# Fourier mixing and a gated feed-forward layer on one core: row E of batch 0 in four column tiles, sines loaded earlier, most weight pieces converted inside the steps

## The chip, the cores and the metric

The kernel runs on one core of a Trainium2 chip. Times are device microseconds of that core. Five engines work side by side, each through its own instructions in order: PE (TensorE, matmuls), ACT (ScalarE), DVE (VectorE), POOL (GpSimd) and SP (SyncE, which here only issues transfers). What one engine needs from another is guarded by semaphores.

## The reference

```python
x: (8, 3008, 256) float32
X = real(fft(fft(x, axis=1), axis=2))             # per batch
t = X.reshape(24064, 256)
out = (sigmoid(t @ w_gate) * (t @ w_val)) @ w_out  # w_gate, w_val: 256 x 1536; w_out: 1536 x 256
```

The three weight matrices arrive as 64-bit floats, because the random float32 values are scaled by a float64 number. The kernel turns them into float32 itself, with integer operations on the two 32-bit halves of each number.

## The kernel before

**The transform.** For one batch, positions 0 to 3007 are folded by symmetry, so that a cosine and a sine sum over a table (`ST[0]`, loaded by `load_table`) give everything: `pk` (cosine part), `qk` (sine part), each 128 features by 1505 frequencies, and one more row for the feature in the middle (feature 128 of 256), called row E here. The table comes in four transfers: two of cosines, two of sines. A sum is made by `seq_group`: twelve matmuls of about 377 columns for `pk` (two blocks, six table slices each), twelve for `qk`. An ACT copy and two DVE additions (`places`) per block bring it out of PSUM.

Row E of batch 0 is made by `seq_group` with `what` = 2. Its left operand is one column broadcast to 128 columns, so the row comes out in all 128 partitions, as tile `ek`. For batches 1 to 7 the rows come out of `e_sums`: seven columns in each of four column tiles of the array, written as one small tile `er`, stored to the DRAM tensor `ed`, and read back by `e_rows` as a broadcast to 128 partitions.

**The weights.** The feature transform is merged into `w_gate` and `w_val`, so each needs the conversion first and four matmuls with the table `dt` afterwards. The conversion is cut into 18 pieces of 512 KB, listed in `jobs` as (matrix, chunk): matrix 0 is `w_gate`, 1 is `w_val`, 2 is `w_out`. A piece goes through:

- `weight_load(j)`: one transfer on SP's queue. Pieces from number `KEEP` = 10 on use three raw buffers in turn, so the load of piece j+3 waits until piece j is converted.
- `weight_parts(j)`: two ACT operations.
- `weight_join(j)`: three DVE operations and then one addition on POOL.
- `weight_use(j)`: for `w_gate` and `w_val` the merge (`merge`): four matmuls into `ps`, two ACT copies into `G2` and `G1`, and two small transfers of row 0 of `G2` into `ge`. For `w_out` it lists the additions of `forms(g)` (`W_SUMS`, `W_COPIES`), which make the 15 weight blocks of one group of three feature tiles. They run on POOL for group 0 and on DVE for the others.

**The steps.** After the head the kernel runs 576 steps: 8 batches, 6 chunks of 252 frequencies, 12 feature tiles of 128. Step i issues, on every engine, in this order: `front_a(i)` (PE: `G1` with `pk`; in steps 0 to 4 of batch 0 also `G2` with row E, which lies as one row of an otherwise zero tile); `part(i)` (from step 5 to 11 two DVE operations that add `ge` times row E, else one ACT operation); `gate_a(i-1)` and `gate_b(i-1)` (ACT sigmoids, three DVE operations, and on POOL seven sums if (i-1) mod 3 is 1, six if it is 2); then the pieces of this step: `pre` (joins of this step, parts of the next step's joins) and `use`, and one entry of the `forms` list; `back` (PE: five matmuls of 168 columns with the weight blocks, from step 5 on); `front_b(i)` (PE: `G2` with `qk`); then what is in `side` for this step, the piece loads among it. Piece chunk c belongs to steps 2c and 2c+1 of the first twelve: `front_a(2c)` reads `G1` of both pieces of chunk c, and from step 5 on `part(2c)` reads their `ge`.

There is no planner: the order on each engine is the order of the calls (`manual_schedule`), and three tuples of step numbers say where the pieces go. Transfers take eight semaphores in turn, and a transfer also waits for the one that used its semaphore before.

Of the kernel before, what the change touches and what calls it, by code (L numbers as in the profile page):

```python
# [7 lines left out]
F32 = mybir.dt.float32  # L8
# [36 lines left out]

NQ = 6
NP = 126  # L50
HP = 64
# [3 lines left out]
              (15, 4, 6, 1)),  # L55
          2: ((11, 8, 11, 0), (12, 8, 12, 0), (9, 5, 9, 0), (10, 10, 5, 0), (16, 2, 11, 0),
              (16, 9, 16, 0))}
W_SUMS = (((1, 3), (5,), 1, 6), ((6, 7), (0, 2), 0, 8), ((4,), (8, 9), 0, 10), ((6,), (2, 3), 1, 12),
          ((0, 2), (1, 3), 0, 14), ((0,), (7,), 1, 16))
W_COPIES = ((2, -1), (0, 1), (4, 1), (5, 1))  # L60

PRODUCTS = ((0, 12), (1, 11), (4, 6), (6, 10), (2, 13), (5, 4), (13, 0),
# [15 lines left out]
def kernel(  # L78
# [10 lines left out]
    nc = tc.nc  # L89
    B, _, _, _, D = xf.shape  # L90
    F = moe_w_gate.shape[1]
    P = 128
# [35 lines left out]
    def mm(o, l, r, start, stop):  # L128
        nc.tensor.matmul(o, l, r, start=start, stop=stop, skip_group_check=True)  # L129
# [72 lines left out]


    assert NPR == 6
    jobs = [(0, 0), (1, 0), (0, 1), (1, 1), (2, 0), (0, 2), (1, 2), (2, 1), (0, 3), (1, 3), (0, 4), (2, 2),
            (1, 4), (0, 5), (1, 5), (2, 3), (2, 4), (2, 5)]
    RAW, WS = {}, {}
    shared = {}
    KEEP = 10
# [47 lines left out]
    def weight_parts(j):  # L257

        if j in RAW:
            raw, ws = RAW[j], WS[j]  # L260
            lo, hi = raw[:, :, :, 0], raw[:, :, :, 1]
            nc.scalar.activation(ws, hi.bitcast(F32), AF.Abs)
            nc.scalar.activation(lo, lo.bitcast(U32), AF.Copy, scale=2.0 ** -29)
# [83 lines left out]
    def fold_ops(b, nq):  # L347
# [58 lines left out]
            first(pool, 2, 3, qs[1])  # L406
            ops += [lambda: half1(qs[0]), lambda: half2(qs[1])]
        for blk, (v, r) in enumerate(parts):
            W[b, blk] = (v[:, :, 0:HD], r[:, :, 0:HD],
                         v[:, :, HD : HD + 1].to_broadcast([v.shape[0], NQ, P]))  # L410
        return ops


# [40 lines left out]

    def seq_start(b):
        PQE[b] = [pqp.tile([P, NK + 1], F32, name=name, tag=name) for name in ("pk", "qk")]
        if not b:
            PQE[b].append(op.tile([P, NK + 1], F32, name="ek", tag="os"))
        for t in PQE[b]:
            nc.vector.memset(t[:, NK:], 0.0)  # L460

    def seq_group(b, blk, what, other=None):
        return half(lambda q: W[b, blk][what][:, q, :], PQE[b][what], blk, what == 1, other)
# [9 lines left out]
        tt(x8[:, :, 1], x8[:, :, 0], x8[:, :, 2], op=ALU.add)  # L473
        tt(x8[:, :, 3], x8[:, :, 0], x8[:, :, 2], op=ALU.subtract)

    def e_sums():


        ps = bank("pe", 0)
        m = B - 1  # L480
        at_ = lambda blk, par: slice((2 * blk + par) * TB, (2 * blk + par) * TB + m)
        for q in range(0, NQ, 2):
            for blk in range(2):
                c0, n = ((0, NE), (NE, NO))[blk]
                for par in range(2):
                    mm(ps[at_(blk, par), 0:n], x8[:, :, 1 + 2 * blk, q + par],
                       ST[0][0:NP, 0, q + par, c0 : c0 + n], q == 0, q == NQ - 2)
        er = op.tile([P, NK + 1], F32, name="er", tag="os")[0:m]
        nc.vector.memset(er[:, NK:], 0.0)
        a = evp.tile([P, NE], F32, name="a", tag="a")[0:m]  # L490
        e1 = evp.tile([P, NE], F32, name="a", tag="a")[0:m]
        nc.scalar.copy(a, ps[at_(0, 1), 0:NE])
        nc.scalar.copy(e1[:, 0:NO], ps[at_(1, 0), 0:NO])

        def rest():
            places(er, 0, True, a, ps[at_(0, 0), 0:NE])
            nc.scalar.copy(a[:, 0:NO], ps[at_(1, 1), 0:NO])  # L497
            places(er, 1, False, e1[:, 0:NO], a[:, 0:NO])
            nc.scalar.dma_start(out=ed[1:], in_=er)
        return rest  # L500


# [40 lines left out]
    def part(i):  # L543

        pqe, ks, n, f, _ = cut(i)
        AP[i] = app.tile([P, 2, CH], F32, name="ae", tag="ae")[:, :, 0:n]
        if not N1 <= i < NFT:
            nc.scalar.activation(AP[i], PF[i], AF.Copy, scale=2.0)  # L548
            return
        for g in range(2):  # L550
            nc.vector.scalar_tensor_tensor(out=AP[i][:, g], in0=pqe[2][:, ks],  # L551
                                           scalar=ge[:, g, f : f + 1], in1=PF[i][:, g],
                                           op0=ALU.mult, op1=ALU.add)

# [131 lines left out]
    for j in range(2):  # L686
        weight_load(j)
    load_x(0)
    for _ in load_table(0, NQ // 2):
        pass  # L690
    for j in range(2, 5):
        weight_load(j)
    sines = load_table(1, NQ // 2)
    next(sines)
    for j in range(5, 7):
        weight_load(j)
# [16 lines left out]

    e0 = shared["qk"][:, 4 * WC : 4 * WC + CH]
    nc.gpsimd.memset(e0, 0.0)
    other = {(0, 0): (4, None), (0, 1): (4, None), (0, 2): (0, 1), (1, 2): (2, 3)}
# [36 lines left out]
    at(N1 - 1, lambda: nc.vector.tensor_copy(PQE[0][1][0:1, 0:CH], PQE[0][2][0:1, 0:CH]))  # L753


    i0 = NFT
# [7 lines left out]
    for i, f in enumerate(mirror_tables()):  # L764
        at(2 * i0 - 2 + i, f)
    at(3 * i0, e_fold)
    at(3 * i0 + 4, lambda: e_sums()())
    at(3 * i0 + 6, table_again)
    for i in range(i0, count, i0):
        at(i - 8, lambda i=i: e_rows(i))  # L770

# [99 lines left out]
```

## Time and profile before

| what | value |
|---|---|
| median of 3 runs | 1973.83 us (1973.28 to 1974.29) |
| the profiled execution itself | 1973.76 us |
| its span, first to last instruction | 1972.0 us |
| PE busy in the span | 1935.8 us, 98% |
| first matmul of the cosine sums | 21.39 us |
| last matmul of the sine sums ends | 46.99 us |
| second half (`front_b`) of step 0, 4, 8, 12 starts | 53.49, 70.60, 93.73, 110.19 us |
| steps from 12 on | about 3.12 us each |

PE is named by the instructions that it executes; one matmul of the program is two records in the trace. Idle time before an instruction stands in brackets with the instruction or transfer that ended it. Everything that the change touches lies in the first 120 us; from step 12 on PE has hardly a gap.

### The profile page before, as it was taken

Reading aid. Unit: us, or ns where it says so; the run is one execution under the profiler, and the core shown is the slowest. Engines: PE = TensorE matmul, PEld = TensorE weight load, DVE = VectorE, ACT = ScalarE, POOL = GpSimd, SP = SyncE. Lnnn points to the kernel's source line nnn. Section 1 sums busy time; section 2 is a strip of 40 time slices with the busy share of each in tenths; the row PEclk is TensorE's granted clock in tenths of the full one; section 3 lists DMA queues with packets and bytes.
Section 4 is the critical chain, followed back from the end, with each engine's and each line's share of the span. In section 5 each row is a group of like instructions: output and inputs, shape, how many; then the busy total and the mean of one; then the engine's idle time right before and its main releaser. Section 6 shows DMA issues by size and latency. Waiting matters only on the chain.

```text
span 1972.0 us, 34403 instructions
## 1 busy us (share of the span) xinstructions
PE 1935.8 (98%) x11252; PEld 1792.4 (91%) x11252; DVE 1511.7 (77%) x3170; ACT 1339.5 (68%) x3108; POOL 1625.0 (82%) x2843
## 2 busy tenths in 40 slices
PE   6999999999999999999999999999999999999997
PEld 4889889999999899998999989999899999999997
DVE  6888778886787677786778867787678776777777
ACT  3567657766777577775777757777577766777775
POOL 3779888997889788996889868998688996777776
PEclk9999999999999999999999999999999999999999
DMA  8363412212022121212012021211210110011011
GB/s 271 86 134 94 138 52 85 51 22 78 14 51 54 17 76 17 72 31 78 14 28 78 14 78 25 47 48 24 78 19 14 21 20 14 14 20 22 14 19 27
DMA packets 171584, 101.41 MB, mean 51 GB/s; under 512 B 133904, under 2 KB 163218, under 8 KB 168602
## 3 DMA queue, kind: packets, MB, share of 16 engines
q1 hardware_dynamic: 169434, 98.64, 20.6%
q8 instruction: 90, 1.47, 0.3%
q10 hardware_dynamic: 1940, 0.56, 0.1%
q14 instruction: 88, 0.72, 0.1%
q0 software_dynamic: 32, 0.00, 0.0%
HBM read 74.45 MB, written 50.18 MB: 63 GB/s over the span
## 4 chain that ended last, share of the span: by engine, by line
PE 95%; DMA 2%; DVE 2%; ACT 1%; issue 0%; POOL 0%; SPq 0%; ACTq 0%; DVEq 0%; POOLq 0%
PE pf L129 49%; PE po L129 41%; PE ev L129 4%; DMA st<-in_stab_dram 1%; PE ps L129 1%; DMA ge<-G 1%; PE od L129 0%; DMA raw<-in_moe_w_val_dram 0%; DMA xr<-in_xf_dram 0%; DVE c L637 0%; DVE ae L551 0%; DVE wf L337 0%; DVE wx L273 0%; ACT z L585 0%; DVE wx L275 0%
## 5 line engine op out<-in xcount | busy, mean ns | idle before, releaser
L590 POOL TENSOR_TENSOR sf<-h 128x168 f32<-128x168 f32 (+1 forms) x960 | 548.8, 590 | 221.6 <-DVE h L586 221.6
L590 POOL TENSOR_TENSOR sf<-h,sf 128x168 f32<-128x168 f32 (+1 forms) x1152 | 657.2, 590 | 60.5 <-DVE h L586 60.5
L129 PE MATMUL pf<-qk,G 128*128 128x252 f32 (+1 forms) x2304 | 582.4, 375 | 3.1 <-DVE ae L551 2.0
L129 PE MATMUL pf<-pk,G 128*128 128x252 f32 (+1 forms) x2304 | 583.4, 376 | 0.0
L586 DVE TENSOR_TENSOR h<-z 128x252 f32<-128x252 f32 (+1 forms) x576 | 299.1, 519 | 356.9 <-ACT z L585 356.6
L532 ACT ACTIVATE pf<-ek,ge 128x252 f32<-128x252 f32 (+1 forms) x1128 | 531.4, 471 | 18.4
L129 PE MATMUL po<-sf,wf 128*128 128x168 f32 (+1 forms) x3072 | 530.1, 305 | 0.0
L548 ACT ACTIVATE ae<-pf 128x504 f32<-128x504 f32 (+1 forms) x569 | 335.0, 589 | 245.6 <-PE pf L129 245.5
L637 DVE TENSOR_TENSOR c<-c 128x168 f32<-128x168 f32 (+1 forms) x949 | 484.3, 541 | 5.5 <-ACT c L614 0.3
L129 PEld LDWEIGHTS pf<-pk,G 128*128 128x128 f32 x2304 | 436.7, 190 | 52.6 <-issue 2.3
L129 PEld LDWEIGHTS po<-sf,wf 128*128 128x128 f32 x3072 | 472.8, 190 | 8.3
L129 PE MATMUL po<-h,wf 128*128 128x168 f32 (+1 forms) x2688 | 477.2, 306 | 1.7 <-ACT a L497 1.6
L129 PEld LDWEIGHTS po<-h,wf 128*128 128x128 f32 x2688 | 428.8, 191 | 19.0 <-ACT a L497 2.0
L129 PEld LDWEIGHTS pf<-qk,G 128*128 128x128 f32 x2304 | 410.2, 190 | 29.2 <-DVE ae L551 2.6
L572 DVE TENSOR_TENSOR z<-ae,pf 128x504 f32<-128x504 f32 (+1 forms) x569 | 377.4, 663 | 21.5 <-ACT h L567 20.9
L567 ACT ACTIVATE h<-pf 128x252 f32<-128x252 f32 (+1 forms) x576 | 217.9, 378 | 164.0 <-PE pf L129 152.9
L585 ACT ACTIVATE z<-z 128x252 f32<-128x252 f32 (+1 forms) x576 | 231.1, 401 | 80.3 <-DVE z L572 60.1
L584 DVE TENSOR_TENSOR h<-h,pf 128x252 f32<-128x252 f32 (+1 forms) x576 | 231.9, 403 | 0.0
L590 POOL TENSOR_TENSOR sf<-sf 128x168 f32<-128x168 f32 (+1 forms) x192 | 111.3, 580 | 15.1
L590 POOL TENSOR_TENSOR sf<-sf,h 128x168 f32<-128x168 f32 (+1 forms) x192 | 106.6, 555 | 0.0
L129 PE MATMUL ev<-st,x 63*128 63x376 f32 (+4 forms) x372 | 98.0, 414 | 8.3 <-DVE x L364 7.8
L129 PEld LDWEIGHTS ev<-st,x 63*128 63x128 f32 (+1 forms) x372 | 66.4, 187 | 36.1 <-DVE x L364 8.2
(120 smaller groups left out, 861.9 us busy)
## 6 DMA issues: line engine op xcount, KB each, us to landing
x<-xr SPq DMA_DIRECT2D x14, 1536.0 KB
out_dram<-os SPq DMA_DIRECT2D x380, 56.0 KB
xr<-in_xf_dram SPq DMA_DIRECT2D x14, 768.0 KB
xr<-in_xf_dram SPq DMA_DIRECT2D x35, 256.0 KB
ek<-ed SPq DMA_DIRECT2D x39, 126.0 KB
out_dram<-os SPq DMA_DIRECT2D x288, 7.0 KB
st<-in_stab_dram SPq DMA_DIRECT2D x4, 1111.9 KB
x<-in_xf_dram SPq DMA_DIRECT2D x2, 1512.0 KB
```

Of the source, the lines that this page charges most:

```text
L129: nc.tensor.matmul(o, l, r, start=start, stop=stop, skip_group_check=True)
L532: nc.scalar.activation(PF[i][:, g], EK[i // NFT], AF.Copy, scale=ge[:, g, f : f + 1])
L548: nc.scalar.activation(AP[i], PF[i], AF.Copy, scale=2.0)
L567: nc.scalar.activation(H[p][:, fh, 0:n], PF[i][:, 0], AF.Sigmoid)
L572: nc.vector.tensor_tensor(z[:, :, ::-1], AP.pop(i), PF[i], op=ALU.subtract)
L584: nc.vector.tensor_tensor(h[:, fh, 0:n], h[:, fh, 0:n], PF.pop(i)[:, 1], op=ALU.mult)
L585: nc.scalar.activation(z[:, 0], z[:, 0], AF.Sigmoid)
L586: nc.vector.tensor_tensor(h[:, fh, n:], z[:, 0], z[:, 1], op=ALU.mult)
L590: nc.gpsimd.tensor_tensor(block(p, dst), block(p, a), block(p, b), op=(ALU.subtract, ALU.add)[op])
L637: engine.tensor_tensor(t[:, dst * R : (dst + 1) * R], *v, op=(ALU.subtract, ALU.add)[op])
```

## The change

It does five things.

1. Row E of batch 0 is made by `e_sums(1, ...)`, the function that made the other seven: one column in each of the four column tiles instead of a broadcast to 128. The result is one row in partition 0. It is copied to the row-E tile for steps 0 to 4 as before; for steps 5 to 11 it goes to `ed` in DRAM and comes back through `e_rows(0)`, called before step 0, as `EK[0]`.
2. In the head the sine table's two transfers are queued ahead of pieces 2 and 3.
3. `jobs` is reordered: `w_val` of chunk 2 comes ahead of the first `w_out` pieces, and pieces 4 to 12 change places.
4. Before step 0 only pieces 2, 3 and 4 are converted, and the ACT part of piece 5 is done; the joins of pieces 5 to 17 stand in steps 0, 1, 1, 2, 3, 4, 5, 5, 6, 7, 8, 8 and 10. Before, pieces 2 to 8 were converted in the head and 9 to 17 in steps 0 to 7 and 9. The merges move with them: chunk 3 in steps 4 and 5 (before 3 and 4), chunk 4 in 6 and 7 (before 5 and 6), chunk 5 in 8 and 9 (before 7 and 8).
5. `W_SUMS` is reordered, so that the blocks that `back` needs first come first.

```diff
-W_SUMS = (((1, 3), (5,), 1, 6), ((6, 7), (0, 2), 0, 8), ((4,), (8, 9), 0, 10), ((6,), (2, 3), 1, 12),
-          ((0, 2), (1, 3), 0, 14), ((0,), (7,), 1, 16))
+W_SUMS = (((1, 3), (5,), 1, 6), ((0,), (7,), 1, 16), ((6,), (2, 3), 1, 12), ((6, 7), (0, 2), 0, 8),
+          ((4,), (8, 9), 0, 10), ((0, 2), (1, 3), 0, 14))
-    jobs = [(0, 0), (1, 0), (0, 1), (1, 1), (2, 0), (0, 2), (1, 2), (2, 1), (0, 3), (1, 3), (0, 4), (2, 2),
-            (1, 4), (0, 5), (1, 5), (2, 3), (2, 4), (2, 5)]
+    jobs = [(w, c) for c in range(3) for w in range(2)] + [(2, 0), (2, 1), (0, 3), (1, 3)]
+    jobs += [(0, 4), (1, 4), (2, 2), (0, 5), (1, 5), (2, 3), (2, 4), (2, 5)]
...
-    def e_sums():
+    def e_sums(m, column, b):
         ps = bank("pe", 0)
-        m = B - 1
...
-                    mm(ps[at_(blk, par), 0:n], x8[:, :, 1 + 2 * blk, q + par],
+                    mm(ps[at_(blk, par), 0:n], column(blk, q + par),
...
-            nc.scalar.dma_start(out=ed[1:], in_=er)
+            nc.scalar.dma_start(out=ed[b : b + m], in_=er)
+            return er
...
-            nc.vector.scalar_tensor_tensor(out=AP[i][:, g], in0=pqe[2][:, ks],
+            nc.vector.scalar_tensor_tensor(out=AP[i][:, g], in0=EK[i // NFT],
...
     sines = load_table(1, NQ // 2)
     next(sines)
-    for j in range(5, 7):
-        weight_load(j)
+    weight_load(2)
     next(sines)
-    for j in range(7, KEEP):
+    for j in range(3, KEEP):
         weight_load(j)
...
-    cos = [seq_group(0, blk, what, other.get((blk, what))) for blk in range(2) for what in (0, 2)]
+    cos = [seq_group(0, blk, 0, (2 * blk + 1, 2 * blk + 2)) for blk in range(2)]
...
-    sin = [seq_group(0, blk, 1, other.get((blk, 1))) for blk in range(2)]
+    e_row = e_sums(1, lambda blk, q: W[0, blk][2][:, q], 0)
+    sin = [seq_group(0, blk, 1, (None, 1 if blk else None)) for blk in range(2)]
...
-    evacuate = [then for _, then, _ in cos + sin]
-    for then, js in zip(evacuate, ((2, 3), (4,), (5,), (6,), (7,), (8,))):
-        weight_round(*js)
+    for _, then, _ in cos:
         then()()
-    nc.scalar.dma_start(out=ed[0:1], in_=PQE[0][2][0:1])
-    nc.vector.tensor_copy(e0[0:1], PQE[0][2][0:1, 0:CH])
-    weight_parts(9)
+    e_row = e_row()
+    weight_round(2)
+    nc.vector.tensor_copy(e0[0:1], e_row[:, 0:CH])
+    for j, (_, then, _) in zip((3, 4), sin):
+        weight_round(j)
+        then()()
+    weight_parts(5)
...
-    for j, i in enumerate((0, 1, 2, 3, 4, 5, 6, 7, 9), 9):
+    for j, i in enumerate((0, 1, 1, 2, 3, 4, 5, 5, 6, 7, 8, 8, 10), 5):
...
-    for j, i in enumerate((0, 0, 1, 2, 0, 3, 4, 5, 4, 6, 7, 8, 8, 8, 11), 3):
+    for j, i in enumerate((0, 1, 2, 2, 2, 4, 5, 6, 7, 6, 8, 9, 9, 9, 11), 3):
         use.setdefault(i, []).append(lambda j=j: weight_use(j))
...
+    e_rows(0)
```

More of the change, by code (lines that the diff above doesn't have):

```diff
@@ L408, in fold_ops @@
         for blk, (v, r) in enumerate(parts):
-            W[b, blk] = (v[:, :, 0:HD], r[:, :, 0:HD],
-                         v[:, :, HD : HD + 1].to_broadcast([v.shape[0], NQ, P]))
+            W[b, blk] = v[:, :, 0:HD], r[:, :, 0:HD], v[:, :, HD : HD + 1]
         return ops
@@ L456, in seq_start @@
         PQE[b] = [pqp.tile([P, NK + 1], F32, name=name, tag=name) for name in ("pk", "qk")]
-        if not b:
-            PQE[b].append(op.tile([P, NK + 1], F32, name="ek", tag="os"))
         for t in PQE[b]:
@@ L485, in e_sums @@
                 for par in range(2):
-                    mm(ps[at_(blk, par), 0:n], x8[:, :, 1 + 2 * blk, q + par],
+                    mm(ps[at_(blk, par), 0:n], column(blk, q + par),
                        ST[0][0:NP, 0, q + par, c0 : c0 + n], q == 0, q == NQ - 2)
[L488 to L493, printed above, removed]
-        def rest():
+        def rest():
+            er = op.tile([P, NK + 1], F32, name="er", tag="os")[0:m]
+            nc.vector.memset(er[:, NK:], 0.0)
+            a = evp.tile([P, NE], F32, name="a", tag="a")[0:m]
+            e1 = evp.tile([P, NE], F32, name="a", tag="a")[0:m]
+            nc.scalar.copy(a, ps[at_(0, 1), 0:NE])
+            nc.scalar.copy(e1[:, 0:NO], ps[at_(1, 0), 0:NO])
             places(er, 0, True, a, ps[at_(0, 0), 0:NE])
@@ L688 @@
     load_x(0)
-    for _ in load_table(0, NQ // 2):
-        pass
-    for j in range(2, 5):
-        weight_load(j)
+    list(load_table(0, NQ // 2))
     sines = load_table(1, NQ // 2)
     next(sines)
-    for j in range(5, 7):
-        weight_load(j)
+    weight_load(2)
     next(sines)
-    for j in range(7, KEEP):
+    for j in range(3, KEEP):
         weight_load(j)
@@ L715 @@
     nc.gpsimd.memset(e0, 0.0)
-    other = {(0, 0): (4, None), (0, 1): (4, None), (0, 2): (0, 1), (1, 2): (2, 3)}
-    cos = [seq_group(0, blk, what, other.get((blk, what))) for blk in range(2) for what in (0, 2)]
+    cos = [seq_group(0, blk, 0, (2 * blk + 1, 2 * blk + 2)) for blk in range(2)]
     for i, f in enumerate(fold_ops(0, NQ // 2)):
@@ L750 @@
             at(i, lambda j=j: weight_load(j + 3))
-    for j, i in enumerate((0, 0, 1, 2, 0, 3, 4, 5, 4, 6, 7, 8, 8, 8, 11), 3):
+    for j, i in enumerate((0, 1, 2, 2, 2, 4, 5, 6, 7, 6, 8, 9, 9, 9, 11), 3):
         use.setdefault(i, []).append(lambda j=j: weight_use(j))
-    at(N1 - 1, lambda: nc.vector.tensor_copy(PQE[0][1][0:1, 0:CH], PQE[0][2][0:1, 0:CH]))
+    at(N1 - 1, lambda: nc.vector.tensor_copy(PQE[0][1][0:1, 0:CH], e_row[:, 0:CH]))
     i0 = NFT
@@ L766 @@
     at(3 * i0, e_fold)
-    at(3 * i0 + 4, lambda: e_sums()())
+    at(3 * i0 + 4, lambda: e_sums(B - 1, lambda blk, q: x8[:, :, 1 + 2 * blk, q], 1)())
     at(3 * i0 + 6, table_again)
+    e_rows(0)
     for i in range(i0, count, i0):
```

## The prediction

> **What bounds it now.** First the page's head and slices.
>
> ```profile
> span 1972.0 us, 34403 instructions
> ...
> PE 1935.8 (98%) x11252; PEld 1792.4 (91%) x11252; DVE 1511.7 (77%) x3170; ACT 1339.5 (68%) x3108; POOL 1625.0 (82%) x2843
> ```
>
> PE is idle 36 us in all, so only PE's work and PE's gaps count. Busy time by stage (columns: stretch, its length, then PE, PEld, DVE, ACT, POOL busy) says where the gaps are:
>
> ```profile
> 0.00:21.40 21.40, 5.14 (x17) 3.97 (x17) 10.44 (x19) 5.22 (x10) 6.83 (x11) 0.92 0.86 306
> 21.40:48.80 27.40, 26.65 (x79) 15.81 (x80) 23.41 (x39) 12.05 (x22) 12.26 (x10) 0.93 0.85 245
> 48.80:75.60 26.80, 24.68 (x114) 21.30 (x113) 20.07 (x35) 16.67 (x44) 20.20 (x25) 1.00 0.36 102
> 75.60:107.00 31.40, 28.13 (x143) 24.90 (x142) 29.68 (x61) 12.51 (x36) 23.30 (x33) 0.95 0.35 102
> ...
> 119.90:200.00 80.10, 80.10 (x472) 74.54 (x474) 64.05 (x129) 57.57 (x135) 69.95 (x123) 1.00 0.53 108
> ```
>
> From 119.9 us PE never rests, so the change is worth what it moves front_b of step 12, now at 110.19. In the head PE bounds (26.65 of 27.40). In steps 5 to 11 DVE does: 29.68 of 31.40. The timeline of steps 3 to 5 shows how a piece holds up PE:
>
> ```profile
> 66.54 1.47 POOL L277 TENSOR_TENSOR wx<-wx 128x512 int32<-128x512 int32 x1
> ...
> 68.03 0.37 SPq L255 DMA_DIRECT2D wx<-in_moe_w_val_dram  x1
> ...
> 71.90 0.68 ACT L262 ACTIVATE wx<-wx 128x512 f32<-128x512 f32 x1 [1.62 <-DMA wx<-in_moe_w_val_dram]
> ...
> 73.29 0.38 ACT L299 COPY G<-ps 128x256 f32<-128x256 f32 x1
> ...
> 73.81 1.96 PE L129 MATMUL ps<-wx,dt 128*128 128x256 f32 x8 [1.35 <-ACT G L299]
> ```
>
> POOL's addition ends (68.01), the load that waited for its buffer is issued, ACT waits 3.87 us for it to land, and ACT's G copies stand behind that. This loop decides my forecast. Finally, row E in column tiles exists already for batches 1 to 7:
>
> ```profile
> L129 PE MATMUL pe<-st,x x24: 477/479/491, 199.0 to 200.6; 126*7 126x377 f32 x12, 126*7 126x376 f32 x12
> ```
>
> **What the skill says.** "TensorEngine Tiling (Array Packing)", Theoretical Speedup: up to 4 times for 32 columns or fewer. The trace agrees: 2.1 us for these twelve matmuls, 7.6 for the broadcast form (25.16 to 27.06, and three stretches like it). "GPSIMD Engine Reference", Key points: POOL shares SBUF interfaces with DVE, and DVE operations in a two-port mode or with two SBUF inputs contend. It does here: a join's first operation takes 0.41 to 1.22 us, its second 0.43 to 1.40. "DMA: Bandwidth & Descriptors", Anatomy of one DMA: about 2.0 us plus bytes/436e9, an estimate of 3.2 us for a piece; the trace's 3.87 is used. "TensorE: Matmul & The Clock Gate", What's actually happening: half rate after an idle window of about 3.4 us. Here 2.0 us sufficed: ten records of po took 2.83 at 104.40 instead of 1.59.
>
> **Head.** The cosine sums still start at 21.39, behind DVE's fold. Without row E between them they end at 30.9 (first half 21.39 to 27.06 with three slow matmuls; the last three wait for POOL's fold, 28.92). Row E takes 2.1, to 33.0. The sines' second half now leaves SP at about 20.3, when the first cosine transfer lands, not at 26.10. At the 0.28 MB/us of these slices, 2.1 MB less ahead of it makes some 7 us: landing near 35.5 instead of 42.88, needed at 36.8, so hidden with 1.3 us to spare. Sine sums end at 40.6 instead of 46.99.
>
> Row E's way out costs 4.2 us (201.07 to 205.2 in the existing form), to 37.2; ACT's parts of piece 2 queue behind it. DVE then has three joins at 1.55 (0.43+0.43+0.69), two held up about 0.5 and one 0.7 by POOL's additions, a copy 0.65, four places 1.8: qk is complete at 46.0. PE's three merges and G2 products end at 46.55: front_b(0) comes 6.9 us sooner than 53.49. Row E through DRAM is due 20 us later and costs nothing; without that cover it would be two transfers of about 2 us.
>
> **Steps 0 to 4.** PE needs 4.27 us a step (2.55 pf, 1.73 ps), as before; step 3 has no merge now and takes up ACT's lag. front_b(4) comes near 63.65 instead of 70.60: the 6.9 is kept.
>
> **POOL falls behind.** Conversions moved out of the head are not gone. ACT, with parts 6 and 7 ahead of it (2.4 us), gives step 0's first sigmoid at 48.85; DVE's gate operations end at 50.6, join 7 at 52.15, join 6 at 54.6, because POOL's addition of piece 7 holds its second operation. From there POOL has back to back: the additions of pieces 6, 8, 9 and 10 at 1.3 (5.2), seven sums 4.3 (60.59 to 65.29 less a wait), six sums 4.05 (67.97 to 72.00), six weight additions 4.4 (53.66 to 56.70, and 1.33): 17.95. So piece 9 is added at 69.75, and PE, ready for its merge at 65.35, idles 4.4; piece 10 is added at 72.55. Before, the fifth in-step addition ended at 75.7, but it was piece 13.
>
> **The loop.** Piece 13's load, on SP, uses piece 10's raw buffer and waits for that addition: it lands at 72.55+3.87 = 76.4. Its parts stand on ACT in step 5, one step after the load (before: two), ahead of the G copies of piece 9; G1 of piece 9 is what front_a(6) reads, and its ge row is sent from G2. So: parts 1.2, copy of G2 0.35, 77.95; ge 0.5 to issue and 1.75 in flight (the chain of waits at 80.20), 80.2; part(6) ends at 80.7, against 82.7 before. Of 6.9, 2.0 are left. Behind ACT's wait also stand step 5's sigmoids, and DVE's gate operations wait for those.
>
> The same two steps on. After part(6): gate operations 1.6 (z 0.6, h 0.55, h 0.45), six sums on POOL 4.05, addition of piece 13 1.3, load of piece 16 3.9, its parts in step 7 1.2, G2 of piece 11 0.35, ge 2.3, half of part(8) 0.5: 15.2. part(8) ends at 95.9, against 92.3: 3.6 lost. PE waits for G1 of piece 11 until 93.4.
>
> Step 8, on DVE: gate 1.6, weight additions 0.8, two joins among POOL's sums at 2.3 (0.76+0.65+0.91 from 79.64), part 0.8: part(9) ends at 103.7, against 96.4. Step 9: z 0.6, then on ACT z 0.55 and the parts of piece 17 1.2, G2 of piece 14 0.35, ge 2.3, half a part 0.5: part(10) at 109.2, against 102.0. Step 10: gate 1.6, weight additions 1.2, a join 2.0, part 0.8: part(11) at 114.8, against 105.5. front_b(11) follows at once; before, PE's half rate held it until 107.06. Step 12 comes 3.12 later, at 118.0.
>
> **The sum** at front_b(12): head -6.9; loss up to part(6) 4.9, to part(8) 5.6, to part(9) 3.7, to part(10) -0.1, to part(11) 2.1; the half rate of before, which had cost it 1.5 there, -1.5: +7.8. The profiled execution took 1973.8 (1.8 of it outside the span, 0.1 below the median): 1981.6, rounded to 1981.5.
>
> **What isn't shown, from both sides.** Joins take 1.55 alone and 3.0 under an addition (70.84 to 73.91): the five in the sum may move it by -3 to +3. PE at half rate after the new gaps: 0 to 1.7; I take 0, as DVE and ACT decide there. The sines on time or 3 late: on time. With every duration clean (sums 0.52, joins 1.55, weight additions 0.68) the same terms give part(6) 79.1, part(8) 93.3, part(9) 99.6, part(10) 105.1, part(11) 109.9: still 2.9 behind at the end.
>
> **Edits at nothing.** W_SUMS: the same additions; group 2's first blocks are ready an entry sooner, worth at most the 0.34 that PE waits for DVE at 116.11. Row E's DRAM way: SP issues its broadcast before step 0, ahead of no load; the ACT issue (0.5) is in the 4.2. The order of w_out's pieces: their blocks are needed from step 5 on, and group 0's are ready in step 4.
>
> **Rivals.**
>
> R1, the loop is there but costs what the head gives: all durations near clean, or POOL starts a little sooner. +2.9 above, less 1 to 5 for waits that overlap: 1972 to 1977. For it: a chain added up by hand counts some waits twice; DVE was busy anyway, so part of the stall replaces it. Against: ACT's 1.62 and PE's 1.35 at 71.90 and 73.81 came with two steps of slack between load and parts, and now there is one.
>
> R2, the other side: loads land before they matter. This is decided at piece 10: were it added right after its join (66.9+1.3 = 68.2), its successor would land at 72.1 and part(6) end at 77, which is when DVE gets there anyway. From part(6) DVE has five joins instead of three: the 5.6 left becomes 1.6 at 2.0 a join, and 3.1 with the half rate gone; clean joins make 5.3: 1968.5 to 1970.7. Against: the 17.95 us that POOL has queued.
>
> R3, it doesn't do what it says: column tiles that don't overlap for one column give 7.6 instead of 2.1, 5.5 later on top of the loop: 1987. The row at 199.0 speaks against.
>
> **Chances.** Loop, +4 to +11: 0.52. R1: 0.24. R2: 0.21. R3: 0.03. 0.2% is 3.9 us, about what a measurement of this kernel can tell from no change. R1 lies within it; R2's 0.21, with a head that may give more, goes to faster; slower is 0.55. The likeliest case's own range is 1977.5 to 1985. For 8 in 10 I leave out R3, the worst of the loop and the best third of R2: 1969 to 1984.5.
>
> **What would show it.** pe at about 31 us in 24 records of 0.48; the last sine matmul at 40 to 41; front_b(0) near 46.6, front_b(4) near 63.7. Then: PE idle some 4 us before piece 9's merge, with POOL as releaser; ACT's first parts operation (L261) waiting for a wx transfer by several us in step 5 and again in step 7; PE's pf waiting for ACT's G copy in steps 6 and 8; front_b(12) near 118. Wrong if ACT never waits for wx, if POOL's addition of piece 10 comes before 69, or if the second sine half lands after 37.

## The result

The changed kernel takes 1986.35 us (median of 4 runs, 1985.06 to 1986.84) against 1973.55 us; the ratio is 1.0065 (95% interval 1.0048 to 1.0083). It is slower by 12.8 us, where 7.7 were forecast; 1986.35 lies 1.85 us beyond the end of the range. Its profiled execution spans 1985.0 us.

The page's head and the busy time by stage of the changed kernel (columns as before: length, then PE, PEld, DVE, ACT, POOL busy, clock, DMA share, GB/s):

```profile
span 1985.0 us, 34403 instructions
...
PE 1938.3 (98%) x11252; PEld 1792.8 (90%) x11252; DVE 1513.7 (76%) x3170; ACT 1339.5 (67%) x3109; POOL 1625.5 (82%) x2843
```

```profile
21.40:48.80 27.40, 26.87 (x104) 16.59 (x103) 18.63 (x34) 11.68 (x24) 8.51 (x7) 0.90 0.96 297
48.80:75.60 26.80, 20.56 (x89) 17.11 (x88) 24.70 (x38) 14.02 (x35) 22.71 (x27) 0.94 0.04 5
75.60:107.00 31.40, 24.30 (x113) 20.89 (x113) 22.50 (x44) 11.33 (x30) 19.23 (x26) 0.92 0.29 86
...
140.00:200.00 60.00, 56.90 (x318) 52.99 (x317) 45.84 (x94) 38.54 (x91) 49.66 (x85) 0.97 0.54 100
```

Two things are to be seen. PE is idle 6.2 us in the second stage (2.1 before) and 7.1 in the third (3.3 before). And between 140 and 200 us, where PE never rested before, 3.1 us are missing.

The loop of addition, load, parts and copies, in the changed kernel's timeline:

```profile
31.52 2.08 PE L128 MATMUL pe<-st,x 126*1 126x377 f32 x24
...
69.86 1.28 POOL L276 TENSOR_TENSOR wf<-wf 128x512 int32<-128x512 int32 x1
...
71.20 3.68 PE L128 MATMUL ps<-wf,dt 128*128 128x256 f32 x8 [4.69 <-POOL wf L276]
...
72.83 1.46 POOL L276 TENSOR_TENSOR wx<-wx 128x512 int32<-128x512 int32 x1
...
74.32 0.38 SPq L254 DMA_DIRECT2D wx<-in_moe_w_gate_dram  x1
...
78.19 0.66 ACT L261 ACTIVATE wx<-wx 128x512 f32<-128x512 f32 x1 [7.75 <-DMA wx<-in_moe_w_gate_dram]
...
79.98 0.69 PE L128 MATMUL pf<-pk,G 128*128 128x252 f32 x2 [2.40 <-ACT G L298]
```

Row E takes 2.08 us in column tiles. PE waits 4.69 us for POOL's addition of piece 9. Piece 10 is added until 74.29, the load of piece 13 leaves at once and lands 3.87 us later, and ACT has waited 7.75 us for it; behind that stand the G copies for which PE waits 2.40 us.

The gap between 140 and 200 us. First timeline lines of the kernel before (SP's queue, and ACT's first read of the row), then those of the changed one:

```profile
85.26 10.71 SPq L301 DMA_DIRECT2D ge<-G  x6
96.07 0.71 SPq L152 DMA_DIRECT2D xr<-zero  x1
...
166.91 5.73 SPq L520 DMA_DIRECT2D ek<-ed  x1
...
181.67 0.98 ACT L532 ACTIVATE pf<-ek,ge 128x252 f32<-128x252 f32 x2
```

```profile
98.03 10.72 SPq L300 DMA_DIRECT2D ge<-G  x4
108.85 0.72 SPq L151 DMA_DIRECT2D xr<-zero  x1
...
179.34 5.44 SPq L516 DMA_DIRECT2D ek<-ed  x1
...
193.25 0.98 ACT L528 ACTIVATE pf<-ek,ge 128x252 f32<-128x252 f32 x2 [3.71 <-DMA ek<-ed]
...
194.28 2.05 PE L128 MATMUL pf<-pk,G 128*128 128x252 f32 x4 [3.10 <-ACT pf L528]
...
199.10 1.01 PE L128 MATMUL pf<-pk,G 128*128 128x252 f32 x4
```

The `ge` transfers of the last merges stand on SP, and SP waits there for ACT's G copies. Only then come the copies of batch 1 (`xr`), small loads, the mirrored tables, and among these the row-E broadcast for step 36. In the changed kernel the `ge` transfers are gone at 108.75 instead of 95.97, 12.8 us later, though the steps are only 8.1 us late. The broadcast is issued until 184.78, and ACT can read the row 8.5 us later. In the kernel before SP has issued it at 172.64; with the same 8.5 us, which is an estimate, the row is there at 181.1, and ACT first reads it at 181.67: some 0.6 us to spare.

So the 13.0 us of the span fall into two parts: `front_b` of step 12 starts at 118.30 instead of 110.19 (8.1), and from there to the end it takes 1866.7 instead of 1861.8 us (4.9). Of these 4.9 the gap itself is 3.1. The step behind it is slow, too: from 194.28 to 199.10 it takes 4.82 us instead of 3.12, and its first four records take 2.05 us instead of 1.01.

### The profile page after: what moved, and what is told of

Same layout as the page of the kernel before. It is cut to its first block, busy times and chain, and to the rows that moved or that the text cites. A ratio compares the mean times of both kernels' runs of the same rounds, so it can differ in the third digit from the quotient of the medians.

```text
span 1985.0 us, 34403 instructions
## 1 busy us (share of the span) xinstructions
PE 1938.3 (98%) x11252; PEld 1792.8 (90%) x11252; DVE 1513.7 (76%) x3170; ACT 1339.5 (67%) x3109; POOL 1625.5 (82%) x2843
## 4 chain that ended last, share of the span: by engine, by line
PE 93%; DVE 2%; DMA 2%; POOL 1%; ACT 1%; issue 0%; SPq 0%; ACTq 0%; DVEq 0%; POOLq 0%
PE pf L128 48%; PE po L128 40%; PE ev L128 4%; DMA ek<-ed 1%; DMA x<-in_xf_dram 1%; POOL sf L586 1%; PE od L128 1%; DVE c L633 0%; POOL wf L333 0%; PE pe L128 0%; DMA wx<-in_moe_w_val_dram 0%; POOL wx L276 0%; DMA ge<-G 0%; DMA wx<-in_moe_w_out_dram 0%; DVE h L582 0%
```

## The experiments

All times by step below are starts of `front_b` in one profiled execution. "0 to 5" is step 5 less step 0; "after 12" is the span less step 12. The ratio is to runs of the kernel before on the same chip, whose medians lie between 1973.49 and 1974.28 us.

| kernel | step 0 | 0 to 5 | 5 to 12 | step 12 | after 12 | median us | ratio to before (95%) |
|---|---|---|---|---|---|---|---|
| before | 53.49 | 23.77 | 32.93 | 110.19 | 1861.8 | 1973.55 | |
| changed | 47.18 | 28.96 | 42.16 | 118.30 | 1866.7 | 1986.35 | 1.0065 (1.0048 to 1.0083) |
| row36_early | 46.35 | 28.75 | 42.49 | 117.59 | 1861.6 | 1981.02 | 1.0037 (1.0025 to 1.0049) |
| loads_ahead | 47.76 | 28.93 | 38.05 | 114.74 | 1866.3 | 1981.59 | 1.0038 (1.0026 to 1.0050) |
| pool_first | 46.77 | 27.59 | 43.09 | 117.45 | 1865.8 | 1984.49 | 1.0057 (1.0042 to 1.0072) |
| copies_first | 45.31 | 29.85 | 37.41 | 112.57 | 1863.6 | 1981.09 | 1.0038 (1.0023 to 1.0053) |
| same_places | 47.19 | 28.50 | 36.75 | 112.44 | 1861.5 | 1974.91 | 1.0008 (0.9999 to 1.0017) |
| steps_alone | 51.42 | 29.42 | 41.90 | 122.74 | 1865.4 | 1991.10 | 1.0098 (1.0082 to 1.0114) |
| head_alone | 48.06 | 32.53 | 32.91 | 113.50 | 1862.3 | 1976.92 | 1.0014 (1.0007 to 1.0020) |
| row_alone | 52.57 | 24.29 | 31.53 | 108.39 | 1861.8 | 1973.66 | 1.0006 (0.9996 to 1.0016) |
| join_light | 46.21 | 27.33 | 34.39 | 107.93 | 1861.5 | 1971.38 | 0.9986 (0.9978 to 0.9995) |
| add_light | 46.11 | 22.48 | 39.16 | 107.75 | 1862.3 | 1971.73 | 0.9991 (0.9982 to 0.9999) |
| mixed_all | 45.87 | 33.70 | 31.13 | 110.70 | 1861.8 | 1974.31 | 1.0005 (0.9996 to 1.0013) |
| early | 50.77 | 30.88 | 32.21 | 113.86 | 1861.4 | 1976.43 | 1.0014 (1.0007 to 1.0021) |
| between_moved | 50.80 | 26.63 | 31.52 | 108.95 | 1861.5 | 1972.21 | 0.9986 (0.9979 to 0.9993) |
| between_kept | 49.78 | 25.93 | 32.92 | 108.63 | 1862.2 | 1972.28 | 0.9984 (0.9977 to 0.9992) |
| before_copies | 52.42 | 24.15 | 32.91 | 109.48 | 1862.2 | 1973.64 | 0.9994 (0.9986 to 1.0002) |

In the eight kernels that have one and the same head (changed, row36_early, loads_ahead, pool_first, copies_first, same_places, join_light, add_light) step 0 lies anywhere from 45.31 to 47.76, so the differences between steps are compared, not single starts. Where only the medians differ by 1 us or less, nothing is concluded.

How far one execution can be trusted is seen in two pairs. Up to step 23 row36_early does just what the changed kernel does; its steps 5 to 7 take 14.96 us against 16.18 and its steps 7 to 12 take 27.53 against 25.98. And the half rate of PE comes and goes: in steps 7 to 12 the kernel before has it once (granted clock 0.92 on average, 21.31 us), row_alone with the same steps does not (1.00, 19.92 us). So differences of some 1.5 us in a stretch can be chance.

### SP's queue and step 36: row36_early

```diff
-        at(i - 8, lambda i=i: e_rows(i))
+        at(i - (13 if i == 3 * i0 else 8), lambda i=i: e_rows(i))
```

> The changed kernel, with the broadcast of row E for step 36 issued on SP after step 23 instead of step 28, ahead of most of the table's mirrored transfers. Theory A (the 3.1 us gap of PE at 194 us, and the half rate after it, come from SP's queue, which the pieces' ge transfers held until 108.75 instead of 95.97): the gap goes, steps up to 35 stay where they are (front_b of step 12 near 118.3), and the time falls by 4.5 to 5 us, to about 1981.5. Rival B (the transfer is slow for the traffic on the DMA rings, not for its place in the queue, or another transfer of the same queue takes over as the late one): no change, 1986, or less than 2 us.

1981.02 us, 5.3 less. The time after step 12 is back at 1861.6, and 0 to 12 is unchanged (71.24 against 71.12). The broadcast's place in row36_early:

```profile
98.40 9.68 SPq L300 DMA_DIRECT2D ge<-G  x4
108.18 0.72 SPq L151 DMA_DIRECT2D xr<-zero  x1
...
162.60 0.55 SPq L516 DMA_DIRECT2D ek<-ed  x1
```

SP is as late as in the changed kernel (108.18), but the row leaves at 162.60, some 26 us before ACT reads it. The 4.9 us are the row's place in SP's queue, and rival B falls.

### Loads, POOL's order and ACT's order, one at a time

loads_ahead gives pieces 13 and 14 raw buffers of the head that are free by then, so that five loads are under way instead of three:

```diff
-            r, i = (j - KEEP) % 3 * 2, 6 + (j - KEEP) % 6
+            r, i = (j - KEEP) % 5 * 2, 6 + (j - KEEP) % 6
...
-        if KEEP <= j < len(jobs) - 3:
-            at(i, lambda j=j: weight_load(j + 3))
+        if j == 7 or KEEP <= j < len(jobs) - 5:
+            at(i, lambda j=j: weight_load(j + (6 if j == 7 else 5)))
+    at(2, lambda: weight_load(14))
```

> The changed kernel, with five raw buffers instead of three for pieces 10 to 17 (the two new ones are buffers of the head that are free by then): pieces 13 and 14 are loaded after steps 1 and 2, pieces 15, 16 and 17 after steps 4, 5 and 5. Nothing else moves. Theory A (the loop of addition, load, parts and G copies sets steps 5 to 11): ACT's waits of 7.75, 2.39 and 2.14 us for piece loads go, the addition of row E for step 6 starts near 77 instead of 80.7, front_b of step 12 comes at 110 to 112 instead of 118.3, and the time is 1973 to 1978. Rival B (DVE and POOL would set these steps at the same pace, with six joins more in the steps; the load was only the last of several equal waits): front_b of step 12 gains at most 2 us, 1984 or more.

1981.59 us: between the two, and neither theory's number. From step 5 to step 7 it takes 10.04 us instead of 16.18: the loop is gone. From 7 to 12 it takes 28.01, about what row36_early takes there (27.53; 25.98 in the changed kernel), where the kernel before takes 21.31. Of 14.4 us that steps 0 to 12 cost more than before, the loads are 4.1.

pool_first lets the joins of steps 3 and 4 go ahead of group 0's weight additions:

```diff
-        for f in [parts_.pop(0)] + todo if parts_ else todo + [lambda: parts_ and parts_.pop(0)()]:
+        for f in [parts_.pop(0)] + todo if parts_ and i >= N1 else todo + [lambda: parts_ and parts_.pop(0)()]:
```

> The changed kernel, with the joins of steps 3 and 4 issued ahead of the weight additions of group 0 in the same step, so that POOL adds pieces 9 and 10 before these additions (0.9 and 0.78 us each). Theory A (PE's 4.69 us before the merge of piece 9 are POOL's queue): that wait falls to 3 us or less, front_b of step 5 comes some 2 us sooner than 76.14, the load of piece 13 leaves at about 71 instead of 74.3, and 2 to 4 us of it last to the end: 1982 to 1984.5. Rival B (DVE, busy 24.7 of 26.8 us there, gives the joins no sooner, so POOL's order does not matter): the wait stays within 1 us of 4.69, and the time within 1 us of 1986.

1984.49 us, within theory A's time, but its interval overlaps that of the changed kernel, so these 1.9 us are not clear of noise. By the trace there is less of the mechanism than theory A asked: PE's wait falls from 4.69 only to 3.33 us, and 0 to 5 by 1.4, of which 0.9 is lost again from step 5 to 12. The 3.33 us that stay are not a matter of this order.

copies_first issues ACT's parts behind the merges' copies of the same step:

```diff
-            pre.setdefault(i - 1, []).append(lambda j=j: weight_parts(j))
+            after_use.setdefault(i - 1, []).append(lambda j=j: weight_parts(j))
...
-        todo = pre.pop(i, []) + use.pop(i, [])
+        todo = pre.pop(i, []) + use.pop(i, []) + after_use.pop(i, [])
```

> The changed kernel, with ACT's parts of the next step's pieces issued after this step's merges and their G copies instead of ahead of them. Nothing else moves. Theory A (ACT's waits for piece loads cost because the G copies stand behind them): the G copies of pieces 9 and 11 no longer wait for a load, PE's waits for ACT's G copies (2.40, 1.89 and 0.83 us) go, front_b of step 12 comes 3 to 5 us sooner than 118.3, and the time is 1980 to 1983.5. Rival B (the sigmoids behind the waiting parts, or DVE, hold the steps up just as long): less than 1.5 us.

1981.09 us, as theory A said (its profiled execution, with step 0 at 45.31, is the fastest of four). Its timeline where the changed kernel had the wait of 7.75 us:

```profile
71.85 1.46 POOL L276 TENSOR_TENSOR wx<-wx 128x512 int32<-128x512 int32 x1
73.34 0.38 SPq L254 DMA_DIRECT2D wx<-in_moe_w_gate_dram  x1
73.47 0.37 ACT L297 COPY G<-ps 128x256 f32<-128x256 f32 x1 [4.01 <-PE ps L128]
73.74 0.38 ACT L298 COPY G<-ps 128x256 f32<-128x256 f32 x1
77.36 0.67 ACT L261 ACTIVATE wx<-wx 128x512 f32<-128x512 f32 x1 [3.24 <-DMA wx<-in_moe_w_gate_dram]
```

The load leaves no sooner, but the copies of piece 9 now run while it is in flight, and 5 to 7 takes 10.13 us. before_copies, the same edit in the kernel before:

> The kernel before with nothing but ACT's parts issued behind the merges' G copies. The changed kernel gained 5.3 us by it because its pieces' loads came late. In the kernel before ACT waits for a load once, 1.62 us at 71.90, and PE waits 1.35 and 0.70 us for ACT's G copies: 0 to 2 us faster, 1971.5 to 1973.8. More than 2.5 us would mean that the order on ACT, not the late loads, was the cause.

1973.64 us against 1974.28 on the same chip, ratio 0.9994 (0.9986 to 1.0002): no difference. The order on ACT costs only where the loads are late.

### Head and steps apart

head_alone is the kernel before with the new row E and the sines ahead of piece 3. The same pieces are converted before step 0, but on DVE all of them now stand behind the cosine places and row E, and pieces 6, 7 and 8 behind the last sine places. steps_alone is the kernel before with the new `jobs`, step tuples and `W_SUMS`. row_alone has only the new row E, with the sines where they were.

head_alone and steps_alone, the core of each:

```diff
-    for j in range(2, 5):
-        weight_load(j)
...
+    weight_load(2)
     next(sines)
-    for j in range(7, KEEP):
+    for j in range(3, KEEP):
...
+    weight_round(2, 3)
+    nc.vector.tensor_copy(e0[0:1], e_row[:, 0:CH])
+    for js, (_, then, _) in zip(((4,), (5,)), sin):
         weight_round(*js)
         then()()
+    weight_round(6, 7, 8)
```

```diff
-    for then, js in zip(evacuate, ((2, 3), (4,), (5,), (6,), (7,), (8,))):
+    for then, js in zip(evacuate, ((), (), (), (2,), (3,), (4,))):
...
-    for j, i in enumerate((0, 1, 2, 3, 4, 5, 6, 7, 9), 9):
+    for j, i in enumerate((0, 1, 1, 2, 3, 4, 5, 5, 6, 7, 8, 8, 10), 5):
```

> The kernel before with only the new head: row E in four column tiles by way of DRAM, and the sines ahead of piece 3. Order of the pieces, conversions before step 0 (2 to 8) and steps of the others as before. Theory A (the head's gain is real and the new places of the conversions lose it): front_b of step 0 at 47 to 48.5, front_b of step 12 at 104 to 106, 1967 to 1970. Rival B (pieces 3 to 9 land later behind the sines, so that conversions held in the head push back step 0 or the first steps; the conversions had to move for the head to gain): front_b of step 0 at 50 or later, 1972 to 1976.

> The kernel before with only the new order of pieces, the new steps of their conversions and the new order of the weight additions; row E as a broadcast in the head, and the sines where they were. Theory A (the steps lose their 15 us whenever step 0 starts): front_b of step 0 near 53, of step 12 near 124.5, and the time 1990 to 1993. Rival B (POOL and the loads are late only because step 0 comes sooner; with the longer head they have 6 us more): front_b of step 12 at 117 to 119, 1982 to 1986.

> The kernel before with row E in four column tiles by way of DRAM, and nothing else: sines, pieces and steps as before. Theory A (the second half of the sines lands at 42.9 and then sets the end of the head, so the two parts of the change gain only together): PE waits for the sine table by some 4 us, front_b of step 0 comes at 51.5 to 53.5 instead of 53.49, 1972 to 1974. Rival B (the 5.5 us of matmuls taken away are gained as they are): front_b of step 0 at 48 to 49.5, 1968 to 1970.

steps_alone takes 1991.10 us, and 71.32 us for steps 0 to 12 (71.12 in the changed kernel): the steps cost the same whenever step 0 starts, as theory A said.

row_alone gains nothing (1973.66). Its PE timeline shows why; the second line is the second half of the sine sums:

```profile
34.97 1.50 PE L128 MATMUL ev<-st,x 126*128 126x377 f32 x4 [1.16 <-DMA st<-in_stab_dram]
...
41.83 0.90 PE L128 MATMUL ev<-st,x 126*128 126x377 f32 x2 [2.82 <-DMA st<-in_stab_dram]
```

Of the 5.5 us of matmuls taken away, 4.0 are spent waiting for the sine table, so the new row gains only with the sines ahead. The sines ahead without the new row were not run; in the kernel before PE waits 0.52 us for them.

head_alone answers for rival B, and more than that: step 0 comes at 48.06, 5.4 us sooner than before, but step 2 comes at 65.24, 3.2 us later than before, and the time is 1976.92. DVE in head_alone:

```profile
55.61 1.39 DVE L272 TENSOR_SCALAR wf<-wf 128x512 int32<-128x512 int32 x1
57.03 0.69 DVE L274 SCALAR_TENSOR_TENSOR wf<-wf 128x512 int32<-128x512 int32 x1
57.64 0.67 DVE L568 TENSOR_TENSOR z<-ae,pf 128x504 f32<-128x504 f32 x1
```

DVE works on pieces 6 to 9 without a break from 48.2 to 57.6, and only then comes step 0's first gate operation, for which the steps wait. The sines are ahead of the pieces on SP's queue: the loads of pieces 4 and 5 leave at 25.84 and 29.03 instead of 20.28 and 24.84, and DVE starts on piece 2 at 37.65 instead of 26.86. A shorter head does not make DVE's work less.

### All mends at once, and what is left: same_places, join_light, add_light

same_places is the changed kernel with loads_ahead, pool_first, copies_first and row36_early together.

> The changed kernel with every cause named so far taken away at once: five raw buffers, joins ahead of group 0's weight additions, parts behind the G copies, row E of step 36 sent after step 23. The pieces keep their steps. Theory A (queues and loads, not the places of the conversions, are what costs): front_b of step 12 at 108 to 111, near 1968 to 1971. Rival B (with seven joins instead of four in steps 5 to 11, DVE sets the pace there): front_b of step 5 gains 2 to 4 us, steps 7 to 12 still take 26 to 28 us instead of 21.3, and the time is 1974 to 1977.

1974.91 us: rival B's time. Together the four mends bring back 11.4 of the 12.8 us. 7 to 12 takes 25.38 (21.31 before), a little less than the 26 to 28 that B said, and against B's forecast step 5 gained hardly anything (75.69, 76.14 in the changed kernel). Four conversions more stand behind step 0, and steps 0 to 12 take 65.25 - 56.70 = 8.6 us more. That is no fixed price for each: 4.7 us are lost in steps 0 to 5, which have one join more (six instead of five), and 3.8 in steps 5 to 12, which have three more. PE's largest waits in same_places:

```profile
70.75 3.32 PE L128 MATMUL ps<-wf,dt 128*128 128x256 f32 x8 [3.31 <-POOL wf L278]
...
100.41 1.12 PE L128 MATMUL pf<-qk,G 128*128 128x252 f32 x4 [3.09 <-DVE ae L549]
```

One is POOL's in step 4, the other DVE's in step 9. Which of the two sets the pace was tried by taking work away:

```diff
-        ts(out=wi, in0=wi, scalar1=3, scalar2=0x3FFFFFF8, op0=ALU.logical_shift_left,
-           op1=ALU.bitwise_and)
+        if j < 5:
+            ts(out=wi, in0=wi, scalar1=3, scalar2=0x3FFFFFF8, op0=ALU.logical_shift_left,
+               op1=ALU.bitwise_and)
```

> same_places with the second of the three DVE operations of a join left out for pieces 5 to 17 (their weights are then wrong): 13 operations of 0.43 to 1.41 us each less on DVE, nothing less elsewhere. Theory B (DVE sets the pace from step 0 to step 11, so what the head gave is spent on the joins moved behind it): front_b of step 12 comes 5 to 9 us sooner than 112.44, 1966 to 1970. Rival (POOL, or the order of merges and copies, sets it): less than 2 us.

```diff
-        nc.gpsimd.tensor_tensor(wi, wi, lo, op=ALU.add)
+        if j < 5:
+            nc.gpsimd.tensor_tensor(wi, wi, lo, op=ALU.add)
```

> same_places with POOL's addition left out for pieces 5 to 17 (the last bits of their weights are then missing): 13 operations of 1.3 us less on POOL. If POOL's queue sets the merge of piece 9 and its additions slow DVE's second operation (1.40 instead of 0.43 us where they overlap): PE's 3.31 us before that merge fall below 1, front_b of step 5 comes 2 to 4 us sooner than 75.69, that of step 12 4 to 8 us sooner than 112.44, 1967 to 1971. If DVE alone sets the pace and POOL's share is small: less than 2.5 us.

join_light gains 3.5 us (1971.38), less than theory B asked: 1.2 of it in steps 0 to 5, 2.4 in 5 to 12. add_light gains 3.2 (1971.73), a little less than was asked, and quite otherwise: PE's wait before piece 9's merge is gone, steps 0 to 5 take 6.0 us less (2 to 4 were forecast), and 2.4 are given back in 5 to 12. So neither engine alone: POOL's additions bind up to step 5, and from there on DVE in the main. Both at once were not left out, so it is not shown that nothing else adds to the 8.6 us. Busy time by stage of add_light:

```profile
48.80:75.60 26.80, 24.01 (x115) 20.23 (x114) 24.49 (x43) 16.12 (x40) 17.88 (x26) 1.00 0.26 65
75.60:107.00 31.40, 26.50 (x127) 22.01 (x126) 28.71 (x60) 14.33 (x40) 15.24 (x26) 0.95 0.27 81
```

PE has 24.01 of 26.80 us again in the second stage (20.56 in the changed kernel), POOL is idle half of the third, and DVE is at 28.71 of 31.40.

### Other places for the pieces: mixed_all and early

Both are same_places with the order of the pieces and the merges' steps of the kernel before (mixed_all also with its `W_SUMS`); the joins, of mixed_all and then of early, which also has the last copy of row E on ACT:

```diff
-    weight_parts(5)
+    weight_round(5)
+    weight_parts(6)
...
-    for j, i in enumerate((0, 1, 1, 2, 3, 4, 5, 5, 6, 7, 8, 8, 10), 5):
+    for j, i in enumerate((0, 1, 1, 2, 2, 3, 4, 4, 5, 6, 7, 9), 6):
```

```diff
+    weight_round(2)
     for _, then, _ in cos:
         then()()
+    weight_round(3)
     e_row = e_row()
-    weight_round(2)
...
-    for j, (_, then, _) in zip((3, 4), sin):
+    for j, (_, then, _) in zip((4, 5), sin):
...
-    for j, i in enumerate((0, 1, 1, 2, 3, 4, 5, 5, 6, 7, 8, 8, 10), 5):
+    for j, i in enumerate((0, 1, 2, 2, 3, 3, 4, 5, 6, 7, 9), 7):
```

> The same as same_places, but with the order of the pieces, the steps of the merges and the order of the weight additions of the kernel before; pieces 2 to 5 are joined in the head, 6 to 13 in steps 0, 1, 1, 2, 2, 3, 4, 4, and 14 to 17 where the kernel before has them. Theory B (it is the joins in steps 5 to 11 and the late merges that cost): front_b of step 5 at 73 to 76, steps 5 to 12 as before (33 us), front_b of step 12 at 106 to 109 and the time 1968 to 1972, below both kernels. Theory A (places do not matter once loads and queues are mended): no better than same_places within 1 us. A third way: eight joins in five steps are too many for DVE, front_b of step 5 at 78 or later, and 1974 or more.

mixed_all takes 1974.31 us, the same as same_places (theory A's "no better within 1 us", though for the third way's reason). With the pieces of steps 5 to 12 where the kernel before has them, these steps take 31.13 us; but with eight joins in steps 0 to 4 those take 33.70, and step 5 comes at 79.57. 6.1 us of that are PE waiting for group 0's weight blocks, POOL's last work there, which now stands behind the pieces' additions. What is taken out of one stretch stands in the other.

> The head of the changed kernel, with pieces 2 and 3 converted while DVE is idle there (between 26 and 38 us), 4, 5 and 6 between row E and the end of the head; order of the pieces of the kernel before, 7 to 13 joined in steps 0, 1, 2, 2, 3, 3, 4 and 14 to 17 as in the kernel before; merges as there; five raw buffers, parts behind the copies, joins ahead of group 0's additions, row E of step 36 sent after step 23; and the row-E copy at the end of step 4 on ACT. Theory B (what counts is how much DVE has left after step 0): front_b of step 0 at 45 to 46.5, of step 5 at 72 to 75, of step 12 at 104.5 to 107.5, and 1967.5 to 1971, faster than both. Against it: pieces 2 and 3 land too late for the idle time and hold up row E, or seven joins in five steps are still too many: front_b of step 12 at 109 or later, 1973 or more.

early takes 1976.43 us, the case against theory B. Piece 2 is converted at 31.1 and piece 3 at 37.3, when they have landed, row E's additions stand behind piece 3 on DVE (38.84), and step 0 comes at 50.77. The DMA engines were busy 0.93 of this stage; DVE's idle time in the head was time in which there was nothing yet to convert.

### Versions between: between_moved and between_kept

This is the kernel before with the new row E, the sines ahead of piece 5 only, copies_first and row36_early; between_moved joins piece 8 in step 1, between_kept in the head. The loads of both, in place of the changed kernel's:

```diff
+    list(load_table(0, NQ // 2))
+    for j in range(2, 5):
+        weight_load(j)
+    list(load_table(1, NQ // 2))
+    for j in range(5, KEEP):
+        weight_load(j)
```

> The kernel before with row E in four column tiles by way of DRAM, the sines ahead of piece 5 instead of pieces 5 and 7, piece 8 joined in step 1 instead of the head, parts behind the G copies, row E of step 36 sent after step 23. Everything else as before: one conversion is moved behind step 0 instead of four. If the moved conversions are what gives the gain back (POOL up to step 5, DVE after it), one of them fits into the 6.7 us that DVE and the 6.6 us that POOL have free in steps 0 to 4: front_b of step 0 at 49 to 50.5, front_b of step 12 less front_b of step 0 at 56 to 58.5, 1969.5 to 1972. If any earlier step 0 is given back for another reason (DVE and POOL have no room at all): step 12 at 109 or later, 1973 or more.

> between_moved with piece 8 still joined in the head, behind the last sine places: no conversion is moved. Pieces 5 to 8 land some 3 us later than in the kernel before. If DVE has to do piece 8 before step 0's gate operations, front_b of step 1 waits for it as in head_alone (2.96 us there): 1971 to 1974, some 1 to 2 us behind between_moved. If the room counts alone: the same as between_moved within 0.7 us.

1972.21 and 1972.28 us against 1974.28 on the same chip; ratios 0.9986 (0.9979 to 0.9993) and 0.9984 (0.9977 to 0.9992). Both are faster than the kernel before, by some 2 us, and they do not differ: with the sines only ahead of piece 5, it does not matter which side of step 0 piece 8 is on. between_moved is 0.2 us above what was expected (step 0 at 50.80, 0.3 late; 58.15 for 0 to 12, as said; step 12 at 108.95, where 109 or later would have meant no room at all). Of the 2.7 and 3.7 us that step 0 gains, step 12 keeps 1.2 and 1.6. In between_moved that is no more than the half rate that the kernel before has in steps 7 to 12 and this execution has not (21.31 and 20.03 us); in between_kept those steps take 21.30. So the 2 us are measured, but the profiles do not show what brings them.

## Why the prediction was right and wrong

**The step that failed** is the first one: "From 119.9 us PE never rests, so the change is worth what it moves front_b of step 12". PE did not rest there because a row arrived 0.6 us ahead of its use, and that row travels behind SP's queue, which is as late as the last `ge` transfer. The merges that move by one step take their `ge` transfers along; my sum followed the pieces' loads on SP, and under "edits at nothing" only batch 0's own broadcast, but not what is queued behind the `ge` transfers. That is 4.9 us, shown by row36_early. With it my 1981.6 would have been 1986.5; 1986.35 was measured. For the same reason it is not so that all that the change touches lies in the first 120 us.

**Head.** Right: `pe` 2.08 us at 31.52 (2.1 at 31), no wait for the sines, the sine sums end at 41.4 (40.6), step 0 at 47.18 (46.6).

**Steps 0 to 4, POOL.** Right: PE's wait before piece 9's merge is 4.69 us (4.4), with POOL as releaser; step 4 at 64.64 (63.65). Piece 10's addition ends at 74.29, 1.7 us later than I had it: POOL's row without a pause begins 0.8 us later, at 55.37, and takes 18.9 us instead of 17.95.

**The loop.** It is there, with its flight of 3.87 us, and ACT waits for loads in steps 5, 6 and 7 (7.75, 2.39 and 2.14 us); the one in step 6, for piece 14, the sum did not have. (In the kernel before the 3.87 us are the flight, not a wait of ACT, as I wrote: ACT's wait there is the 1.62 of the line.) The ends of the row-E additions: step 6 at 82.1 (80.7), 8 at 96.7 (95.9), 9 at 105.2 (103.7), 10 at 110.1 (109.2), 11 at 114.5 (114.8); step 12 at 118.30 (118.0), so +8.1 where the sum said +7.8.

**What I made of the loop** was too much. "This loop decides my forecast" holds for 4 to 6 of the 14.4 us that steps 0 to 12 lose. The other 8.6 stay when queues and loads are mended, and join_light and add_light bring back 3.5 and 3.6 of them. That points to the work on the conversions itself, though both left work out of 13 pieces and not of the four that moved. The sum had the durations of this work in it and so came out right, but R2, "loads land before they matter", was priced at 1968.5 to 1970.7. With the loads ahead the kernel takes 1981.59 us, or some 1977 less the 4.5 us that it still loses after step 12, and with all mends 1974.91. R2's wrong term is "part(6) end at 77": with the loads there in time the first row-E addition of step 6 starts at 78.60, because POOL had already cost 4.69 us. The half rate, which I took at 0, is seen three times by step 12: piece 9's merge takes 3.68 us instead of 1.9, and the merge at 87.42 (2.88) and the pf records at 105.26 (1.96 instead of 1.12) are slow, too. How much of it lies on the path of the steps was not tried; in so far it is in part luck that the sum was right within 0.3 us.

**Signs and chances.** Slower was the likeliest (0.55). The end at 1984.5 left out "the worst of the loop"; it was not the loop that went beyond it, but a cost that I had not listed at all.

## What to carry to other kernels

Taking work off the bounding engine ahead of a stage gains nothing if the work that other engines do there is only moved behind the gain: count what each engine must have done by a fixed point (here step 5), not where its instructions stand. When an instruction moves, follow its transfers on the issuing queue to the last reader of whatever is queued behind them, even 100 us on; "no gap there now" may hold by 0.6 us. And on an engine with one order, put what others wait for ahead of what may itself wait for a load.

## What was not expected

- Step 5 hardly comes sooner. Step 0 starts anywhere from 45.31 to 53.49 us, but step 5, at 77.26 in the kernel before, comes between 74.36 and 77.43 in ten of the others, and at 79.57 to 81.65 in head_alone, steps_alone, mixed_all and early. Only the two that leave work out reach it sooner: 73.54 in join_light, 68.59 in add_light.
- POOL's additions cost more than the waits that bear POOL's name. In same_places PE waits 3.7 us for them in steps 0 to 4 (3.31 and 0.41), but without the six of these steps 0 to 5 takes 6.0 us less. Most of the rest is PE's clock: behind the wait of 3.31 us the merge takes 3.32 us instead of the 1.99 at 63.74, and the next po records 2.00 instead of 1.59, 1.7 us in all. The stretch from step 0 to step 5, in same_places and then in add_light (the third figure from the end is the granted clock):

```profile
47.19:75.69 28.50, 22.99 (x100) 19.11 (x98) 25.34 (x40) 18.17 (x44) 21.92 (x27) 0.94 0.22 56
```

```profile
46.11:68.59 22.48, 20.81 (x99) 17.89 (x98) 19.21 (x34) 16.23 (x39) 13.51 (x21) 1.00 0.28 68
```

- POOL's additions slow DVE, too: in head_alone the second DVE operation of a join takes 1.39 us at 55.61, under POOL's addition of 55.37 to 56.71, where another takes 0.43, as "GPSIMD Engine Reference", Key points, of the Trainium skill has it: the two engines share their way to SBUF. How much this adds to PE's wait was not measured by itself.
- Not settled: why steps 7 to 12 take 25.4 to 28.0 us in the changed kernel and its variants with the mends, and 21.3 before: the three joins more, the two loads that are still late in loads_ahead and the merges' later steps were not tried apart; and which part of the two between brings their 2 us, since row_alone and before_copies show no difference by themselves.
